# Block-sparse attention and a SoLU layer: start-up buffers, batch 1's order around a root, and the loads of the last two batches on ScalarE's queue

## The chip, the core and the metric

The kernel runs on one core of one Trainium2 chip. The metric is the device time of one execution in microseconds, from the runs shown; a second source is one profiled execution, whose records (the trace) say when each instruction of each engine started and ended, what it waited for, and when each DMA landed.

The engines work side by side and meet at semaphores: TensorE (PE; its weight loads are PEld), VectorE (DVE), ScalarE (ACT), GpSimd (POOL) and SyncE (SP). Each runs its own instructions strictly in order. SP and ACT can also issue DMAs; a DMA's issue is an instruction in the issuing engine's queue like any other.

## The reference

Two stages. Block-sparse attention over 4 batches, 8 heads, 768 positions, head size 64; then a SoLU layer over all 3072 rows:

```
scores = (q @ k.T) / sqrt(64)                 # masked per block of 32: window, edges, 3 random blocks
attn   = exp(scores - max) / (sum + 1e-9)
x      = attn @ v                             # reshaped to rows of 512
h      = x @ w_in                             # 512 -> 1024
solu   = h * softmax(h)
ln     = (solu - mean) / sqrt(var + 1e-6) * g_ln
out    = ln @ w_out                           # 1024 -> 512
```

The mask is the same for all heads and batches.

## The kernel before

Everything is cut into 144 slots. A pass is two blocks of 128 queries of one batch (12 passes, three per batch); a slot within a pass is one pair of heads and one third of the keys, so a pass has 12 slots. For each slot PE computes the scores (`scores`, L393: four matmuls of 256 columns into one of two PSUM tiles called sco), ACT takes the exponential of 1024 columns (`exps`, L407), and PE multiplies it with v (`outs`, L415). The mask rides along as 24 further rows of the transposed keys and queries (KT, QT), so no engine applies it. After the three slots of a pair, DVE takes a reciprocal and writes the normalised result xb (`normalise`, L435).

The SoLU layer of a pass runs during the next passes. xb is transposed by DMA (`x_turn`, xT; for the first pass on PE, `x_first`), then for each block of 128 rows: h on PE (`h_mms`), exp on ACT (`e_exp`, tile e), h times e on DVE (`solu`), a DMA transpose (`ln_turn`, lnT), statistics on DVE (`stats`), the root on POOL (`rstd`, L507, a power of -1/2), the last matmuls on PE (`o_mms`), a scaling on DVE (`scaled`, tile ot) and the store.

The inputs of a batch come as 12 loads of 384 KB (k, q and v of four pairs of heads, `load`, L309; batch 0 has the q loads split). They land in a ring of 7 staging tiles, POOL casts them to bf16 (`cast`). For batch 0 PE transposes k and q (`turn_mm`) and DVE copies them out (`turn_out`, L355); for later batches a DMA transposes them (`turn_dma`, tiles pd_k and pd_q) and POOL copies them into place (`shift`). KT, QT and VA exist twice and are used by alternate batches, and `mask_rows` puts the mask rows into the second copy once.

The order is written by hand. `at(when, fn, ...)` notes a step with a time in slots, and `emit` (L292) calls the steps sorted by that time; each engine gets its instructions in that order. So a number such as 30.05 places a step behind everything at or before 30.05 on its own engine, and nothing moves it later. The lists `first` (batch 1, L761) and `then` (batches 2 and 3, L766) hold the times of loads, casts, transposes, shifts, v loads and v casts; `t0` adds 36 slots per batch. Before the change all loads but the very first are issued from SP, whose queue also carries every DMA transpose and nearly every store.

The steps that the prediction follows: the filler matmuls that keep PE busy at the start (`zeros`, L600, tiles warm and warm_t), the mask tile m_ps and the copies of its rows to QT (L664), the loads of w_in (issued from POOL, L706), the first h matmul, and in slots 27 to 39 the roots, the mask copies (L735) and the casts of batch 1.

Of the kernel before, what the change touches and what calls it, by code (L numbers as in the profile page):

```python
# [7 lines left out]
FP32 = mybir.dt.float32  # L8
# [200 lines left out]
def kernel(  # L209
# [11 lines left out]
    nc = tc.nc  # L221

    B, H, S, D = q.shape
# [3 lines left out]
    TQ = 128  # L227
    NCH = S // TQ
# [11 lines left out]
    KR = D + NB  # L240
    PAIR = 2 * NCH
    PC = 2
    QW = PC * TQ
# [29 lines left out]
    KT = [fix.tile([128, H * NCH, TQ], BF16, name=f"KT{i}") for i in range(2)]  # L273
# [8 lines left out]
    p_sco = work.enter_context(tc.tile_pool(name="p_sco", bufs=2, space=bass.MemoryType.PSUM))  # L282
    p_op = work.enter_context(tc.tile_pool(name="p_op", bufs=1, space=bass.MemoryType.PSUM))
    p_h = work.enter_context(tc.tile_pool(name="p_h", bufs=1, space=bass.MemoryType.PSUM))
# [4 lines left out]
    def at(when, fn, *args):  # L289
        plan.append((when, len(plan), fn, args))  # L290
# [9 lines left out]
    def natural(b, pr, key):  # L300
        if key == "q":
            return qn[:, pr].rearrange("p c (h d) -> p c h d", h=2)
        r = KR if b == 0 and pr else D
        x0 = NCH * 2 * (D + (pr - 1) * KR) if pr else 0
        return kn[:, x0 : x0 + NCH * 2 * r].rearrange("p (c h r) -> p c h r", h=2, r=r)
# [12 lines left out]
    def copy(eng, o, i):  # L318
        if eng is nc.scalar:
            nc.scalar.copy(out=o, in_=i)  # L320
        else:
            eng.tensor_copy(out=o, in_=i)  # L322

    def cast(eng, b, pr, key, c0=0, c1=NCH, l0=None):
        l0 = c0 if l0 is None else l0
        st = stage[key, b, pr, l0].rearrange("p h (c d) -> p h c d", d=D)[:, :, c0 - l0 : c1 - l0, :]
        if key == "v":
            o = VA[b % 2][:, 2 * pr : 2 * pr + 2, c0:c1, 0:D]
        else:
            o = natural(b, pr, key)[:, c0:c1, :, 0:D].rearrange("p c h d -> p h c d")  # L330
        copy(eng, o, st)
# [23 lines left out]
    def turn_out(b, pr, key, engs, c0=0, c1=NCH):  # L355
        tp = turned.pop((key, b, pr, c0))
        dst = (KT if key == "k" else QT)[b % 2]
        for hh in range(2):
            h = 2 * pr + hh
            n, i = D, tp[hh * D : (hh + 1) * D] if len(tp.shape) == 2 else None  # L360
            if i is None:
                n, i = KR, tp[0:KR, hh]
            copy(engs[hh], dst[0:n, h * NCH + c0 : h * NCH + c1, :],
                 i[:, c0 * TQ : c1 * TQ].rearrange("p (c t) -> p c t", t=TQ))

    turned = {}

# [19 lines left out]
    def unit(s):  # L387
        ps, r = divmod(s, SLOTS)
        pr, u = divmod(r, UP)
        b, j = divmod(ps, NPB)  # L390
        return ps, b, j, pr, u
# [163 lines left out]
    DVE2 = (nc.vector, nc.vector)  # L555

    with tc.manual_schedule():
# [4 lines left out]
                          in_=bass.AP(tensor=_t32, offset=0, ap=[[2 * NR, NB], [1, 2 * NR]]))  # L562
# [7 lines left out]
        zer = fix.tile([128, 512], BF16, name="zer")  # L570
# [29 lines left out]
        def zeros(n, pool=p_o):  # L600
            w = pool
            if pool in (p_o, p_op):
                w = pool.tile([128, 512], FP32, tag="o" if pool is p_o else "op", name="warm")
            for _ in range(n):
                nc.tensor.matmul(w, zer[:, 0:128], zer, start=True, stop=True,
                                 skip_group_check=True)

        zeros(8)

        samp_f = fix.tile([NB, NR], FP32, name="samp_f")  # L610
        nc.vector.tensor_copy(out=samp_f, in_=samp_i[:, :, 0])
# [10 lines left out]
        for pr in range(1, NP):  # L622
            nc.scalar.activation(
                out=natural(0, pr, "k")[:, :, :, D:KR].rearrange("p c h r -> p (c h) r"),
                in_=zer[:, 0 : NCH * 2 * NB].rearrange("p (x r) -> p x r", r=NB),
# [1 line left out]
        cast(nc.scalar, 0, 0, "k", 0, 2, 0)  # L627
        cast(nc.scalar, 0, 0, "q", 0, 2, 0)
        cast(nc.scalar, 0, 0, "k", 2, NCH, 0)
        warm_t = p_sco.tile([128, 2, 512], FP32, tag="sco", name="warm_t")[:, 0, :]  # L630
        turn_mm(0, 0, "k", p_h, 0, 2)
        m_ps = p_sco.tile([TQ, 2, 512], FP32, tag="sco", name="m_ps")
        sel_f = selT.rearrange("p c t -> p (c t)")
        for i, x0, x1 in ((0, 0, QW), (1, QW, S)):
            nc.tensor.matmul(m_ps[0:KR, i, 0 : x1 - x0], mask_l, sel_f[:, x0:x1],
                             start=True, stop=True)
# [4 lines left out]
        def spread(x, n):  # L641
            return x.rearrange("p (o c) -> p o c", o=1).broadcast_to([NB, n, x.shape[-1]])
# [7 lines left out]
        def selector(pr):  # L650
            for base, sg in ((0, 1), (BLK - 1, -1)):
                o = natural(0, pr, "k")[:, :, :, D:KR]
                nc.gpsimd.affine_select(out=o, in_=o, compare_op=ALU.is_ge, fill=0.0, base=base,
                                        channel_multiplier=NCH * sg,
                                        pattern=[[sg, NCH], [0, 2], [-BLK * sg, NB]])
# [2 lines left out]
        mask_rows(nc.vector, KT[0], 0)  # L658
        turn_mm(0, 0, "q", p_o, 0, 2)
        turn_mm(0, 0, "k", p_op, 2, NCH)  # L660
        zeros(2, warm_t)
        turn_out(0, 0, "k", DVE2, 0, 2)
        for h0, n, i, x0, x1 in ((0, 2, 0, 0, QW), (0, 1, 1, QW, S), (1, 1, 1, QW, S)):
            nc.scalar.copy(out=rows(QT[0], h0, h0 + n)[:, :, x0:x1],  # L664
                           in_=spread(m_ps[D:KR, i, 0 : x1 - x0], n))
# [6 lines left out]
        scores(1)  # L672
        turn_mm(0, 1, "k", p_h)
        turn_mm(0, 1, "q", p_o, 0, 2)
        turn_out(0, 1, "k", DVE2)
        turn_out(0, 1, "q", DVE2, 0, 2)


        def turn(when, b, pr, key, pool, c0=0, c1=NCH, engs=DVE2, later=0.02):
            at(when, turn_mm, b, pr, key, pool, c0, c1)  # L680
            at(when + later, turn_out, b, pr, key, engs, c0, c1)
# [8 lines left out]
        for pr, w0, w1, w2 in ((2, 1.85, 2.805, 1.01), (3, 4.805, 5.805, 2.9)):  # L690
            at(w2, mask_rows, nc.vector, QT[0], 2 * pr)
            selector(pr)
            cast(nc.gpsimd, 0, pr, "k")
            cast(nc.gpsimd, 0, pr, "q", 0, 2)
            turn(w0, 0, pr, "k", p_h)
            turn(w1, 0, pr, "q", p_o, 0, 2)
        for pr in range(NP):
            at(2.0 + 0.1 * pr, cast, nc.gpsimd, 0, pr, "v")
            at(2.15 + 0.1 * pr, cast, nc.gpsimd, 0, pr, "q", 2, NCH)
        for pr, when in enumerate((8.9, 10.9, 12.9, 15.4)):  # L700
            turn(when, 0, pr, "q", p_o, 2, NCH, later=0.06)
        for n, when in ((2, 0.9), (1, 2.9), (1, 3.9)):
            at(when, zeros, n, p_op)
# [28 lines left out]

        at(2.05, w_load_in)
        at(9.0, w_load_out, 0, KF)
        for n, when in enumerate((7.0, 7.1, 13.1, 14.6, 16.1, 17.6, 30.2, 34.2)):  # L735
            at(when, mask_rows, nc.gpsimd if n < 2 else nc.vector, (KT[1], QT[1])[n % 2],
               2 * (n // 2))
        for c in range(KF):
# [7 lines left out]
        for s in range(n_units):  # L746
            ps, b, j, pr, u = unit(s)
# [10 lines left out]
        srcs = {"k": k, "q": q, "v": v}  # L758
        kq = [(key, pr) for pr in range(NP) for key in "kq"]
        vs = [("v", pr) for pr in range(NP)]  # L760
        first = (  # L761
# [4 lines left out]
        then = (  # L766
# [4 lines left out]
        for b in range(1, B):  # L771
            loads, casts, turns, shifts, v_loads, v_casts = first if b == 1 else then
            t0 = SLOTS * NPB * (b - 1)
            for (key, pr), t_l, t_c in zip(kq + vs, loads + v_loads, casts + v_casts):
                at(t0 + t_l, load, nc.sync, srcs[key], b, pr, key)
                at(t0 + t_c, cast, nc.gpsimd, b, pr, key)
            for (key, pr), t_t, t_s in zip(kq, turns, shifts):
                at(t0 + t_t, turn_dma, b, pr, key)
                at(t0 + t_s, shift, b, pr, key)


        def layer(ps, i, hs, es, os):
            for when, n0, n1 in hs:
                at(when, h_mms, ps, i, n0, n1)
            at(es, e_exp, ps, i)
            head = ps == 0 and i == 0
            at(es + (0.33 if head else 0.5), solu, ps, i)
            at(es + 0.55, ln_turn, ps, i)
            at(es + (6.6 if head else 3.4 if ps == 0 else 1.7), stats, ps, i)
            at(es + (6.7 if head else 3.5), rstd, ps, i)  # L790
            for when, n0, n1 in os:
                at(when, o_mms, ps, i, n0, n1)
            at(os[-1][0] + 0.1, scaled, ps, i, nc.vector)
            at(os[-1][0] + 0.12, store, ps, i)

        LP = NPASS - 1
        for ps in range(LP):
            b0 = SLOTS * (ps + 1)
            at(b0 + (1.9 if ps == 0 else -0.1), x_first if ps == 0 else x_turn, ps)
            if ps == LP - 1:  # L800
                break
            for i in range(PC):
                hs = b0 + 6 * i
                os = hs + (12 if ps == LP - 2 and i == PC - 1 else 14)
                layer(ps, i,
                      [(hs + 3.9, 0, 2), (hs + 4.85, 2, 3), (hs + 5.86, 3, 5), (hs + 6.85, 5, 7),
                       (hs + (7.79 if hs == SLOTS else 7.85), 7, 8)], hs + 8.5, [(os + 0.84, 0, 7), (os + 1.83, 7, 8)])


        ps, b0 = LP - 1, SLOTS * LP  # L810
# [177 lines left out]
```

## Time and profile before

| | us |
|---|---|
| median of 3 runs | 213.5 (211.46 to 215.09) |
| the profiled run's time | 212.79 |
| its span, first to last instruction | 211.1 |
| exps, 144 on ACT | 141.8 busy, 1.025 each |
| scores, 576 matmuls on PE | 86.4 busy |
| outs, 1152 matmuls on PE | 51.8 busy |
| h and o, 153 and 167 matmuls on PE | 48.8 and 41.8 busy |
| DMA issue to landing: loads of k, q, v | 5.4, 5.4, 6.1 (medians) |
| the same: lnT, xT, pd_k, pd_q | 4.1, 3.8, 2.8, 4.8 (medians) |

The granted clock of TensorE was 0.997 in the mean. In the page's lines, a group is given by line, engine and operation, written tile from read tile, shapes and count, then busy time and mean; after the last bar stands the idle time of the engine just before these instructions, and what ended it. In a timeline the two first numbers are the start and the length in us; the bracket at the end is the idle time before and what ended it. A queue with a q (SPq, ACTq) shows the sequencer's own work, such as issuing a DMA. PE's busy time counts matmuls that overlap, so it says more about waiting than about speed.

### The profile page before, as it was taken

Reading aid. Unit: us, or ns where it says so; the run is one execution under the profiler, and the core shown is the slowest. Engines: PE = TensorE matmul, PEld = TensorE weight load, DVE = VectorE, ACT = ScalarE, POOL = GpSimd, SP = SyncE. Lnnn points to the kernel's source line nnn. Section 1 sums busy time; section 2 is a strip of 40 time slices with the busy share of each in tenths; the row PEclk is TensorE's granted clock in tenths of the full one; section 3 lists DMA queues with packets and bytes.
Section 4 is the critical chain, followed back from the end, with each engine's and each line's share of the span. In section 5 each row is a group of like instructions: output and inputs, shape, how many; then the busy total and the mean of one; then the engine's idle time right before and its main releaser. Section 6 shows DMA issues by size and latency. Waiting matters only on the chain. (4 is left out here: it accounts for less than half of the span.)

```text
span 211.1 us, 5628 instructions
## 1 busy us (share of the span) xinstructions
PE 198.1 (94%) x2205; PEld 137.7 (65%) x2238; DVE 138.7 (66%) x329; ACT 176.0 (83%) x208; POOL 108.6 (51%) x154
## 2 busy tenths in 40 slices
PE   7899799998999999999999999999799999999991
PEld 2589667675666676676576676677476676665451
DVE  6785858968756557468548467557448557558782
ACT  6899779878889889889889889889779889876470
POOL 7799598788954483776353674594240110011111
PEclk9999999999999999999999999999999999999998
DMA  5999999999999879999998999989923285427404
GB/s 151 351 361 231 308 385 272 214 198 305 232 201 269 186 170 304 210 136 348 173 248 207 204 201 299 167 193 299 166 72 99 51 103 104 70 79 121 118 15 144
DMA packets 74291, 42.03 MB, mean 199 GB/s; under 512 B 56212, under 2 KB 69780, under 8 KB 74260
## 3 DMA queue, kind: packets, MB, share of 16 engines
q1 hardware_dynamic: 73316, 40.06, 82.2%
q0 software_dynamic: 528, 1.05, 2.8%
q10 hardware_dynamic: 416, 0.52, 0.8%
q8 instruction: 18, 0.29, 0.6%
q14 instruction: 13, 0.11, 0.2%
HBM read 23.07 MB, written 6.29 MB: 139 GB/s over the span
## 5 line engine op out<-in xcount | busy, mean ns | idle before, releaser
L411 ACT ACTIVATE exs<-sco 128x1024 bf16<-128x1024 f32 x144 | 141.8, 1025 | 10.2 <-PE sco L400 6.5
L400 PE MATMUL sco<-QT,KT 88*128 88x256 bf16 x576 | 86.4, 272 | 2.0 <-ACT QT L664 0.8
L400 PEld LDWEIGHTS <-KT 88*128 88x128 bf16 x576 | 55.1, 97 | 33.7 <-issue 5.3
L428 PE MATMUL op<-VA,exs 128*128 128x65 bf16 x1152 | 51.8, 194 | 0.3 <-DVE xb L442 0.2
L470 PE MATMUL h<-w_in_sb,xT 128*128 128x512 bf16 x153 | 48.8, 379 | 2.8 <-DVE solu L491 0.8
L428 PEld LDWEIGHTS <-exs 128*128 128x128 bf16 x1152 | 48.7, 97 | 3.5 <-DVE xb L442 0.7
L530 PE MATMUL o<-w_cen_sb,lnT 128*128 128x512 bf16 x167 | 41.8, 379 | 1.3 <-DMA lnT<-solu 1.1
L523 POOL TENSOR_TENSOR rstd<-vpe,mhalf 128x1 f32<-128x1 f32 x24 | 13.2, 549 | 49.3 <-DVE vpe L521 44.2
L441 DVE RECIPROCAL recip_all<-op 128x4 f32<-128x4 f32 x48 | 8.7, 182 | 41.5 <-PE op L428 41.1
L479 ACT ACTIVATE e<-h 128x1024 bf16<-128x1024 f32 x22 | 22.5, 1024 | 13.6 <-PE h L470 6.4
L505 DVE BATCH_NORM_STATS2 stats<-solu 128x6 f32<-128x512 bf16 x48 | 30.6, 680 | 0.0
L491 DVE TENSOR_TENSOR solu<-h,e 128x1024 bf16<-128x1024 f32 x22 | 26.8, 1216 | 4.1 <-ACT e L479 4.1
L322 POOL COPY KT<-pd_k 64x768 bf16<-64x768 bf16 x24 | 20.2, 840 | 13.1 <-DMA pd_k<-kn 12.3
L322 POOL COPY QT<-pd_q 64x768 bf16<-64x768 bf16 x24 | 19.8, 823 | 12.7 <-DMA pd_q<-qn 11.8
L530 PEld LDWEIGHTS <-lnT 128*128 128x128 bf16 x176 | 15.7, 98 | 14.9 <-DMA lnT<-solu 1.6
L541 DVE TENSOR_SCALAR ot<-o,rstd 128x512 f32<-128x512 f32 x20 | 15.0, 751 | 13.6 <-issue 6.8
L442 DVE TENSOR_TENSOR xb<-op,recip_all 128x256 bf16<-128x256 f32 x48 | 20.4, 425 | 1.7
L470 PEld LDWEIGHTS <-xT 128*128 128x128 bf16 x176 | 15.3, 98 | 6.6 <-DMA xT<-xb 2.0
L322 POOL CAST qn<-st_q 128x768 bf16<-128x768 f32 (+2 forms) x19 | 14.2, 747 | 6.2 <-DMA st_q<-in_q_dram 6.0
L322 POOL CAST kn<-st_k 128x768 bf16<-128x768 f32 x15 | 12.4, 826 | 8.4 <-DMA st_k<-in_k_dram 8.2
L322 POOL CAST VA<-st_v 128x768 bf16<-128x768 f32 x16 | 13.2, 831 | 4.6 <-DMA st_v<-in_v_dram 4.1
L717 POOL TENSOR_SCALAR w_out_sb<-w_out_f,g_ln_sb 128x512 bf16<-128x512 f32 x8 | 6.3, 802 | 2.5 <-DMA w_out_f<-in_moe_w_out_dram 2.5
(87 smaller groups left out, 111.0 us busy)
## 6 DMA issues: line engine op xcount, KB each, us to landing
st_v<-in_v_dram SPq DMA_DIRECT2D x16, 384.0 KB, 6.1
out_dram<-ot SPq DMA_DIRECT2D x23, 256.0 KB, 3.9
st_k<-in_k_dram SPq DMA_DIRECT2D x15, 384.0 KB, 5.4
st_q<-in_q_dram SPq DMA_DIRECT2D x12, 384.0 KB, 5.4
w_out_f<-in_moe_w_out_dram SPq DMA_DIRECT2D x4, 512.0 KB, 11.9
st_q<-in_q_dram SPq DMA_DIRECT2D x4, 256.0 KB, 7.1
w_in_sb<-in_moe_w_in_dram POOLq DMA_DIRECT2D x1, 1024.0 KB, 12.4
st_q<-in_q_dram SPq DMA_DIRECT2D x4, 128.0 KB, 4.9
```

The lines of the kernel that those rows point to most:

```text
L322: eng.tensor_copy(out=o, in_=i)
L400: nc.tensor.matmul(sco[:, hh, kk * QW : (kk + 1) * QW], KT[b % 2][0:KR, h * NCH + 2 * u + kk, :], QT[b % 2][0:KR, h * NCH + PC * j : h * N ...
L411: nc.scalar.activation(out=exs_of[ps, pr][:, u].rearrange("p a b c -> p (a b c)"), in_=sco_of.pop(s).rearrange("p a b -> p (a b)"), func=A ...
L428: nc.tensor.matmul(op[:, hh, ic, :], exs[:, u, hh, kk, ic * TQ : (ic + 1) * TQ], VA[b % 2][:, 2 * pr + hh, 2 * u + kk, :], start=(u == 0 a ...
L442: nc.vector.tensor_tensor(out=xb_of[ps][:, :, 2 * pr * D : 2 * (pr + 1) * D].rearrange("p c (h d) -> p h c d", h=2), in0=op[:, :, :, 0:D], ...
L470: nc.tensor.matmul(h_of[ps, i][:, half, :], xT_of[ps][:, i * KD + c, :], w_in_sb[:, c, half * HF : (half + 1) * HF], start=(c == 0), stop= ...
L479: nc.scalar.activation(out=o, in_=h, func=ACT.Exp, scale=1.0, accum_out=esum_all[:, t : t + 1])
L491: nc.vector.tensor_mul(out=so, in0=h, in1=e)
L505: nc.vector.bn_stats(out=stat_of[ps, i][:, half, :], in_=so[:, half, :])
L523: nc.gpsimd.tensor_tensor(out=rstd_of[ps, i], in0=vpe, in1=mhalf, op=ALU.pow)
L530: nc.tensor.matmul(ops_of[ps, i], lnT_of[ps, i][:, c, :], w_cen_sb[:, c, :], start=(c == 0), stop=(c == KF - 1), skip_group_check=True)
L541: nc.vector.tensor_scalar(out=o, in0=i_, scalar1=r, scalar2=None, op0=ALU.mult)
```

## The change

Four parts.

The start: the eight filler matmuls write a tile of the score pool instead of the o pool, the two fillers before the first scores become four of half the width and write an unused half of the mask tile's first bank, and the copies of the transposed k of pairs 1 to 3 of batch 0, one per head with all 768 columns, become one for both heads with the first 256 columns and, behind the q copies, one for both heads with the other 512 (`k_out`).

The middle of batch 0: the last q turn goes from slot 15.4 to 15.9 and `x_first` from 13.9 to 14.4; the mask rows of pair 3 of the second KT and QT go from 30.2 and 34.2 to 39.0 and 39.5.

Batch 1: casts of k3, q3 and v1 go from 27.6, 27.7 and 28.5 to just behind the root at 30.0, the shifts of k2 and q2 from 30.05 and 30.1 to 30.1 and 30.15, a transpose from 33.0 to 33.2, and the scaling and store of the first block of rows from slot 27.9 to 29.87.

Batches 2 and 3: their 24 loads are issued from ScalarE's queue, at the same times of the plan.

```diff
+    def k_out(pr, c0, c1):
+        tp = turned["k", 0, pr, 0]
+        nc.vector.tensor_copy(
+            out=KT[0][0:KR].rearrange("p (h c) t -> p h (c t)", c=NCH)[
+                :, 2 * pr : 2 * pr + 2, c0 * TQ : c1 * TQ],
+            in_=tp[0:KR, :, c0 * TQ : c1 * TQ])
...
-        zeros(8)
+        warm_t = p_sco.tile([128, 2, 512], FP32, tag="sco", name="warm_t")[:, 0, :]
+        zeros(8, warm_t)
...
-        zeros(2, warm_t)
+        for _ in range(4):
+            nc.tensor.matmul(m_ps[:, 0, QW : 2 * QW], zer[:, 0:128], zer[:, 0:QW], start=True,
+                             stop=True, skip_group_check=True)
...
-        turn_out(0, 1, "k", DVE2)
+        k_out(1, 0, 2)
         turn_out(0, 1, "q", DVE2, 0, 2)
+        k_out(1, 2, NCH)
...
-            turn(w0, 0, pr, "k", p_h)
+            at(w0, turn_mm, 0, pr, "k", p_h)
+            at(w0 + 0.02, k_out, pr, 0, 2)
             turn(w1, 0, pr, "q", p_o, 0, 2)
+            at(w1 + 0.03, k_out, pr, 2, NCH)
...
-        for pr, when in enumerate((8.9, 10.9, 12.9, 15.4)):
+        for pr, when in enumerate((8.9, 10.9, 12.9, 15.9)):
...
-        for n, when in enumerate((7.0, 7.1, 13.1, 14.6, 16.1, 17.6, 30.2, 34.2)):
+        for n, when in enumerate((7.0, 7.1, 13.1, 14.6, 16.1, 17.6, 39.0, 39.5)):
...
-            [9.1, 9.2, 9.3, 9.4, 9.5, 9.6, 27.06, 27.07], [9.5, 9.6, 14.0, 14.1, 14.2, 14.3, 27.6, 27.7],
-            [12.5, 12.6, 24.05, 24.06, 27.1, 27.2, 33.0, 36.1],
-            [17.0, 17.1, 26.0, 27.3, 30.05, 30.1, 36.6, 39.0],
-            [9.7, 27.08, 27.3, 27.4], [18.0, 28.5, 32.0, 33.0])
+            [9.1, 9.2, 9.3, 9.4, 9.5, 9.6, 27.06, 27.07], [9.5, 9.6, 14.0, 14.1, 14.2, 14.3, 30.05, 30.06],
+            [12.5, 12.6, 24.05, 24.06, 27.1, 27.2, 33.2, 36.1],
+            [17.0, 17.1, 26.0, 27.3, 30.1, 30.15, 36.6, 39.0],
+            [9.7, 27.08, 27.3, 27.4], [18.0, 30.07, 32.0, 33.0])
...
-                at(t0 + t_l, load, nc.sync, srcs[key], b, pr, key)
+                at(t0 + t_l, load, nc.sync if b == 1 else nc.scalar, srcs[key], b, pr, key)
...
-            at(os[-1][0] + 0.1, scaled, ps, i, nc.vector)
-            at(os[-1][0] + 0.12, store, ps, i)
+            out_at = 29.87 if head else os[-1][0] + 0.1
+            at(out_at, scaled, ps, i, nc.vector)
+            at(out_at + 0.02, store, ps, i)
...
-            at(b0 + (1.9 if ps == 0 else -0.1), x_first if ps == 0 else x_turn, ps)
+            at(b0 + (2.4 if ps == 0 else -0.1), x_first if ps == 0 else x_turn, ps)
```

More of the change, by code (lines that the diff above doesn't have):

```diff
@@ L359, in turn_out @@
             h = 2 * pr + hh
[L360 to L364, printed above, removed]
+            copy(engs[hh], dst[0:D, h * NCH + c0 : h * NCH + c1, :],
+                 tp[hh * D : (hh + 1) * D, c0 * TQ : c1 * TQ].rearrange("p (c t) -> p c t", t=TQ))
+    def k_out(pr, c0, c1):
[4 more added lines that the diff above has]
+            in_=tp[0:KR, :, c0 * TQ : c1 * TQ])
     turned = {}
@@ L629 @@
         cast(nc.scalar, 0, 0, "k", 2, NCH, 0)
-        warm_t = p_sco.tile([128, 2, 512], FP32, tag="sco", name="warm_t")[:, 0, :]
         turn_mm(0, 0, "k", p_h, 0, 2)
```

## The prediction

> **What bounds it.** I read the page first, then the waits by engine, then the stretches, then the timelines around each wait of TensorE.
>
> ```profile
> PE 198.1 (94%) x2205; PEld 137.7 (65%) x2238; DVE 138.7 (66%) x329; ACT 176.0 (83%) x208; POOL 108.6 (51%) x154
> ```
>
> TensorE is busy 94% of the span; ScalarE, which gets the loads, 83%. A busy PE is not a PE at its peak, so the stretches matter more (us, then busy time of each engine, granted clock, DMA share, GB/s):
>
> ```profile
> 72.43:80.11 7.68, 7.63 (x89) 5.39 (x89) 4.69 (x12) 6.93 (x10) 5.98 (x8) 1.00 0.86 204
> 149.46:158.45 8.99, 8.25 (x90) 5.62 (x92) 4.68 (x12) 7.04 (x10) 2.19 (x3) 1.00 0.55 99
> ```
>
> These are six slots each, from one exps to the sixth after it. In the first PE fills 7.63 of 7.68 us; from exps 45 to exps 141 nearly every period is 7.67 to 7.70. So the floor is PE's own work, and only what exceeds 7.68 can be won: I find 0.6 in exps 27 to 33, 0.7 in 33 to 39, 0.5 in 39 to 45, 0.25 in 75 to 81, 1.3 in 111 to 117 (the second line) and 0.4 in 135 to 141. The waits of PE (total, times, longest) say on whom:
>
> ```profile
> PE o L530 <- DMA lnT<-solu: 1.1, 2, 0.9
> PE h L470 <- DVE solu L491: 0.8, 1, 0.8
> PE h L470 <- DMA w_in_sb<-in_moe_w_in_dram: 0.4, 1, 0.4
> ```
>
> **The beginning.** As built, scores(0) no longer waits for all three copies of the mask rows (L664, 5.62 to 7.17 us) but for the first, at about 6.2; the second score tile takes over the wait for the last. Exps(0) is then held by ScalarE's own copies, to about 7.2 instead of 7.85: 0.65 us won. The fillers are the same columns (2 x 512 become 4 x 256): 0. The split copies put 512 of 1536 columns of each k pair ahead of the q copies: the pair of 88x768 copies took 1.02 us, so about 0.4 us stands ahead of q in place of 1.02, and some 0.4 of the 0.65 lives on. Then it meets a wall: in PE's timeline the first h matmul stands at 26.34, on w_in's DMA.
>
> ```profile
> 25.35 0.60 PE L400 MATMUL sco<-QT,KT 88*128 88x256 bf16 x4
> 26.34 0.38 PE L470 MATMUL h<-w_in_sb,xT 128*128 128x512 bf16 x1 [0.38 <-DMA w_in_sb<-in_moe_w_in_dram]
> ```
>
> That DMA is issued from POOL at 13.88, after casts that wait for loads and for neither PE nor ScalarE, and it lands at the same 26.3. PE only arrives earlier and waits longer. The same holds for moving the turn of q3 behind one group of scores (its 0.37 us wait for DVE goes). Net 0; bounds -0.4 (the landing moves too) and +0.3 (a dearer copy shows). The cover is the w_in wait.
>
> **The root and batch 1.** On POOL the second root (rstd) now stands ahead of the casts of k3, q3 and v1; on DVE the first ot stands behind a reciprocal and xb, and two mask copies (0.55 us each) go from 48.17 and 52.06 to after slot 38's xb. DVE's and PE's timelines:
>
> ```profile
> 44.86 0.75 DVE L541 TENSOR_SCALAR ot<-o,rstd 128x512 f32<-128x512 f32 x1 [1.57 <-POOL rstd L523]
> 48.17 0.55 DVE L647 COPY KT<-selT 24x1536 bf16<-24x1536 bf16 x1
> ```
> ```profile
> 46.22 0.68 PE L428 MATMUL op<-VA,exs 128*128 128x65 bf16 x16 [0.17 <-DVE xb L442]
> 50.59 0.60 PE L470 MATMUL h<-w_in_sb,xT 128*128 128x512 bf16 x2 [0.77 <-DVE solu L491]
> ```
>
> DVE sat 1.57 us before ot while xb, which PE wanted, was queued behind. With xb first PE starts its outs at 45.88 (the scores before it at 45.44 take 0.435), not 46.22: 0.34. Solu at 49.32 stands behind that delay and the mask copy, 0.8 us together; it then ends before PE needs the bank: 0.77. The third place is h at 58.79, 0.35 on xT: xT can go some 0.7 us earlier, but a mask copy now stands before the solu that frees the bank (solu ended at 58.01, now +0.57), so I take 0.2. POOL: kn3's cast moves from 47.30 to about 48.2, the k2 shifts no later than their 51.20, since the root is out of the way. What is late next is the pair-3 shift of q (59.60 to 61.31, wanted by the scores at 62.39): 1.1 us of cover. Sum -1.3; bounds -1.7 and -0.4.
>
> **The 24 loads: the queue left.** SP's queue in the last batches, then PE's wait:
>
> ```profile
> 140.00 1.64 SPq L313 DMA_DIRECT2D st_v<-in_v_dram x3
> 143.30 1.24 SPq L496 DMA_TRANSPOSE lnT<-solu  x1
> ```
> ```profile
> 150.00 1.68 PE L530 MATMUL o<-w_cen_sb,lnT 128*128 128x512 bf16 x7 [0.91 <-DMA lnT<-solu]
> ```
>
> This lnT took 6.7 us from issue to landing; the median is 4.1. Four loads were ahead of it. On ScalarE they are reached after exps 99, 100 and 101 (134 to 137 us), 4 us sooner, and are through before 143. That period's excess of 1.3 us (0.91 here, the rest at the h behind it) goes: -1.3; bounds -1.3 and 0. By the Trainium skill ("DMA: Bandwidth & Descriptors", Issuing engines are not separate DMA queues) another issuer saves only the issuing time, which SP has to spare: by that rule this term would be 0 and the sum 1.3 higher, which is "nothing left" below. This trace speaks against it: the lnT did wait behind loads on its own queue.
>
> **The 24 loads: the queue entered.** Each stands after exps 39, 40, 41, 41, 51, 52, 53, 53, 63, 64, 65, 65 and the same plus 36, so in the three that run back to back after an e. SP paid 0.40 to 0.85 us per load from 59 us on. ScalarE's sequencer runs ahead of its engine:
>
> ```profile
> 0.92 1.28 ACT L250 ACT_TABLE_LOAD   x1 [0.92 <-PEq L972]
> 0.96 0.44 ACTq L313 DMA_DIRECT2D st_k<-in_k_dram  x1
> ```
>
> The issue ran inside the table load. An exps lasts 1.02 us and the next starts 0.90 to 1.04 after it, so one issue of 0.5 is covered; two after exps 41 take 1.1 and make the next some 0.1 to 0.2 late. The scores of slot s+2 start 0.05, 0.22, 0.46, 0.56 us after exps(s) ends (first to fourth after an e), which covers that. So 0; upper bound by SP's transpose issues (1.24 us), below.
>
> Queued behind a load are all later exps. Each load waits for its buffer's cast (done slots before) and, as built, for the DMA eight places before it, which shares its semaphore. Most of those landed long before; the thin ones are v0 and k3 of batch 2 (they wait for an xT and a pd_q that landed at 73.97 and 74.88; ScalarE gets there at 74.3 and 74.8) and their like 36 and 48 slots on. Landings half a us later would still be covered by the 0.56.
>
> **Loads beside transposes.** Before, FIFO kept the loads behind the boundary's transposes; now they run together. Landing to use, in the trace: xT 0.05 to 0.7 us, lnT 0.04 to 3.9. What a foreign packet does is seen here (GB/s in 40 slices of 90 to 94 us):
>
> ```profile
> GB/s 218 212 212 193 67 5 0 10 95 207 202 195 195 371 138 41 3 0 0 0 0 0 0 5 10 8 10 10 8 10 18 251 294 289 292 255 287 289 289 287
> ...
> q8 instruction: 1, 0.02, 1.5%
> ...
> lnT<-solu SPq DMA_TRANSPOSE x1, 4.5
> ```
>
> One instruction fetch, and the transposes stand for 1.5 us. Lower bound 0. Upper: all four loads of a cluster (about 1.05 us each by their landings, 4.2) pass its last transpose; against slacks of 0.05 to 2.7 that is up to 2 us in each of six clusters, +12. I take one load's time per cluster, as the nearest row is FIFO behind one load: it shows where slack is under 1.05, at exps 63 (lnT, 0.8), 75 (xT 0.05, and the q shift at 108.25 for scores at 108.69) and 99 (xT): 0.25 + 0.95 + 0.3, say +1.5.
>
> The same page (Queues, rings and completion order) has each DMA engine take turns between queues by whole packets; by that rule lnT would pass among the loads and the term would lie under +1.5. No transpose of this trace ran beside a load of another queue.
>
> **Sum.** The profiled run took 212.79 us (span 211.1 and 1.7 around it). 0 - 1.3 - 1.3 + 0 + 1.5 = -1.1: 211.7. The median of the runs is 0.7 above the profiled run, so 212.4.
>
> **Rivals.**
> *ScalarE held* (slower): a load at the head of its queue stops the exps. If an issue beside SP's transposes takes their 1.24 us, the exps of a cluster come 0.4, 0.8 and 2.3 us late (1.24 and some 0.06 of waits against 0.90 each; the pair adds 1.5), and against 0.22, 0.46 and 0.56 plus 0.14 of room PE loses about 1.7: six clusters 10, less 2.6: 221. It decides from about 0.75 us per issue, where the pair overruns 1.04 + 0.56. For: SP issues transposes without a break at 72 to 76 and 86 to 91. Against: at 0.96 both queues issued at once in 0.44.
> *Transposes late* (slower): 1.5 us in each cluster, 9 less 2.6: about 219; half of that, 215. For: the stall above. Against: most lnT have 1 to 3 us.
> *Nothing left*: what DVE gives back is eaten by xT, the next in line, and the loads were hidden anyway: 213.5. For: xT lands within 0.2 us of its use at five of eight boundaries.
> *All won*: no contention, w_in lands early, the 0.25 at exps 81 goes too: -0.4 -1.7 -1.3 -0.3 -0.6 (xT) = 208.5 to 209.2.
> That the loads don't come sooner is not a case: they stand 3 to 5 us ahead of SP's times.
>
> **Numbers.** Forecast 0.46; nothing left 0.20; all won 0.07; ScalarE held 0.12; transposes late 0.15, half of it over the bound. A change under about 2% (209.2 to 217.8) can't be told from none here. Faster 0.05, within 0.75, slower 0.20. Range 209.5 to 218.5, leaving out most of "all won", of "ScalarE held" and the worst of the transposes; the forecast's own range is 211 to 214.
>
> **What would show it.** PE without waits at 46 and 50, and at the o after the last v loads; h still waiting for w_in at about 26.3, now over 0.38; exps intervals of 0.90 across each load issue of about 0.5 us. Wrong, if exps wait for a DMA, if an issue on ScalarE's queue lasts over 0.75, or if PE waits for lnT, xT or a q shift at 79, 94, 105 or 108 us.

## The result, and the profile after

| | us |
|---|---|
| before, median of 4 runs | 213.56 (211.46 to 215.09) |
| after, median of 4 runs | 234.9 (232.99 to 237.95) |
| ratio | 1.1005, 95% interval 1.0872 to 1.1139 |
| profiled run after, its span | 234.52, 232.9 |

Slower by 10%, far outside the range. The ratios, here and below, compare the executions within about 1.5% of each kernel's fastest, and the medians are of all. Lines of the changed kernel stand 4 to 10 further down: exps is L415, scores L404, outs L432, h L474, o L534, the xT transpose L457, lnT L500.

The page's table of engines after:

```profile
PE 206.9 (89%) x2240; PEld 141.5 (61%) x2240; DVE 137.2 (59%) x329; ACT 175.3 (75%) x208; POOL 107.0 (46%) x154
```

TensorE now idles for 26 us of its span instead of 13, and its busy time itself rose by 8.8 us for the same matmuls (198.1 before; of the 35 records more, 33 are matmuls that the trace of before lacks and 2 are fillers cut in half). Both need a cause. The waits of PE, then those of ScalarE (total, times, longest):

```profile
PE sco L404 <- ACT exs L415: 7.6, 5, 4.1
PE o L534 <- DMA lnT<-solu: 6.5, 4, 3.2
PE h L474 <- DMA xT<-xb: 2.6, 1, 2.6
PE h L474 <- DMA w_in_sb<-in_moe_w_in_dram: 1.4, 1, 1.4
```
```profile
ACT exs L415 <- DMA pd_q<-qn: 4.8, 1, 4.8
ACT exs L415 <- DMA pd_k<-kn: 2.5, 1, 2.5
...
ACT QT L670 <- PE m_ps L666: 0.9, 1, 0.9
```

The transposes lnT and xT come late (PE waited 1.1 and 0.35 us for them before), and twice an exps, which reads nothing that a DMA brings, waits for the transpose of a q or k. PE's timeline places the waits:

```profile
61.33 0.60 PE L474 MATMUL h<-w_in_sb,xT 128*128 128x512 bf16 x2 [2.59 <-DMA xT<-xb]
85.31 1.01 PE L404 MATMUL sco<-QT,KT 88*128 88x256 bf16 x4 [4.12 <-ACT exs L415]
108.78 1.69 PE L534 MATMUL o<-w_cen_sb,lnT 128*128 128x512 bf16 x7 [2.32 <-DMA lnT<-solu]
143.86 2.58 PE L534 MATMUL o<-w_cen_sb,lnT 128*128 128x512 bf16 x7 [3.21 <-DMA lnT<-solu]
```

Each stands behind one of the six clusters of loads. The stretches (six slots each, columns as before the change: us, busy time of each engine, granted clock, DMA share, GB/s):

```profile
56.23:68.92 12.69, 9.93 (x91) 6.42 (x92) 5.90 (x14) 7.03 (x10) 7.37 (x10) 0.87 1.06 228
76.60:90.39 13.79, 9.67 (x88) 6.36 (x87) 4.39 (x10) 6.82 (x10) 6.28 (x10) 0.75 1.18 203
106.82:116.91 10.09, 8.13 (x91) 5.70 (x92) 4.68 (x12) 7.04 (x10) 5.62 (x8) 1.00 0.87 168
141.00:153.67 12.67, 9.81 (x91) 6.20 (x92) 4.70 (x12) 7.05 (x10) 5.48 (x8) 0.87 0.71 131
153.67:164.00 10.33, 8.52 (x88) 5.89 (x87) 4.83 (x10) 6.85 (x11) 4.05 (x6) 0.88 1.04 273
170.00:177.70 7.70, 7.70 (x90) 5.42 (x89) 4.70 (x12) 6.95 (x9) 2.19 (x3) 1.00 0.60 132
```

Without loads a stretch still takes 7.7 us (last line). The five above it, each with a wait of 1.8 us or more, take 10 to 14. In four of them the same 88 to 91 matmuls are busy for 8.5 to 9.9 us at a granted clock of 0.75 to 0.88. In the third line, whose wait is the 2.32 us at 108.78, the clock stays 1.00. Two pieces of the first two stretches show what the mean hides:

```profile
62.60:65.90 3.30, 3.30 (x27) 2.10 (x24) 1.00 (x5) 1.92 (x2) 1.64 (x2) 0.50 1.17 259
83.10:89.80 6.70, 4.49 (x31) 2.98 (x31) 0.00 (x0) 3.39 (x4) 3.96 (x6) 0.50 1.22 191
```

The trace's clock records have four such pieces at 0.50 before the kernel's end, three of 3.4 us and this one of 6.8, each beginning in a wait or within 1.5 us of its end. So most of these waits are paid twice, as idle time and as slower matmuls behind it.

How exps 54 came to wait for pd_q is seen in ScalarE's timeline with its queue:

```profile
78.36 0.38 ACTq L313 DMA_DIRECT2D st_v<-in_v_dram  x1
78.41 1.04 ACT L415 ACTIVATE exs<-sco 128x1024 bf16<-128x1024 f32 x1
83.76 0.38 ACTq L313 DMA_DIRECT2D st_k<-in_k_dram  x1
84.24 1.94 ACT L415 ACTIVATE exs<-sco 128x1024 bf16<-128x1024 f32 x2 [4.80 <-DMA pd_q<-qn]
```

The load of k3 stands between the exps. In the trace it has the same semaphore as this pd_q, the DMA that the prediction put eight places before it, and it waits for it. That transpose's issue ended at 77.26 and it landed at 83.67, 6.4 us later. The load is issued at 83.76, and only then go the exps queued behind it. An issue itself takes 0.37 to 0.66 us on ScalarE.

### The profile page after: what moved, and what is told of

Its sections match the earlier page's. It is cut to its first block, busy times and chain, and to the rows that moved or that the text cites. A ratio compares the mean times of both kernels' runs of the same rounds, so it can differ in the third digit from the quotient of the medians.

```text
span 232.9 us, 5692 instructions
## 1 busy us (share of the span) xinstructions
PE 206.9 (89%) x2240; PEld 141.5 (61%) x2240; DVE 137.2 (59%) x329; ACT 175.3 (75%) x208; POOL 107.0 (46%) x154
## 3 DMA queue, kind: packets, MB, share of 16 engines
q0 software_dynamic: 528, 1.05, 2.4%
## 4 chain that ended last, share of the span: by engine, by line
PE 59%; DMA 28%; DVE 4%; POOL 3%; ACT 1%; issue 1%; SPq 1%; ACTq 0%; POOLq 0%; DVEq 0%
PE sco L404 20%; PE o L534 13%; PE h L474 13%; PE op L432 11%; DMA lnT<-solu 10%; DMA w_in_sb<-in_moe_w_in_dram 6%; DMA pd_k<-kn 4%; DMA pd_q<-qn 3%; DMA xT<-xb 3%; DMA st_k<-in_k_dram 2%; PE he L851 1%; POOL kn L322 1%; DVE solu L495 1%; POOL kn L657 1%; DVE stats L509 1%
## 5 line engine op out<-in xcount | busy, mean ns | idle before, releaser
L415 ACT ACTIVATE exs<-sco 128x1024 bf16<-128x1024 f32 x144 | 141.1, 1024 | 30.6 <-PE sco L404 18.5
L404 PE MATMUL sco<-QT,KT 88*128 88x256 bf16 x576 | 89.4, 278 | 8.8 <-ACT exs L415 7.6
L404 PEld LDWEIGHTS <-KT 88*128 88x128 bf16 x576 | 56.5, 99 | 43.4 <-issue 17.2
L474 PE MATMUL h<-w_in_sb,xT 128*128 128x512 bf16 x176 | 57.0, 389 | 4.0 <-DMA xT<-xb 2.6
L432 PE MATMUL op<-VA,exs 128*128 128x65 bf16 x1152 | 53.1, 196 | 0.0
L534 PE MATMUL o<-w_cen_sb,lnT 128*128 128x512 bf16 x176 | 46.9, 390 | 6.5 <-DMA lnT<-solu 6.5
L432 PEld LDWEIGHTS <-exs 128*128 128x128 bf16 x1152 | 50.1, 99 | 3.2 <-ACT exs L415 0.4
L322 POOL COPY KT<-pd_k 64x768 bf16<-64x768 bf16 x24 | 20.0, 832 | 34.2 <-DMA pd_k<-kn 33.0
L534 PEld LDWEIGHTS <-lnT 128*128 128x128 bf16 x176 | 16.1, 100 | 21.1 <-DMA lnT<-solu 7.0
L474 PEld LDWEIGHTS <-xT 128*128 128x128 bf16 x176 | 15.9, 100 | 8.6 <-DMA xT<-xb 3.1
L322 POOL CAST qn<-st_q 128x768 bf16<-128x768 f32 (+2 forms) x19 | 13.5, 713 | 0.8 <-DMA st_q<-in_q_dram 0.3
L726 POOL TENSOR_SCALAR w_out_sb<-w_out_f,g_ln_sb 128x512 bf16<-128x512 f32 x8 | 5.7, 721 | 3.3 <-DMA w_out_f<-in_moe_w_out_dram 3.2
## 6 DMA issues: line engine op xcount, KB each, us to landing
st_q<-in_q_dram SPq DMA_DIRECT2D x4, 384.0 KB, 10.3
```

The lines of the kernel that those rows point to most:

```text
L404: nc.tensor.matmul(sco[:, hh, kk * QW : (kk + 1) * QW], KT[b % 2][0:KR, h * NCH + 2 * u + kk, :], QT[b % 2][0:KR, h * NCH + PC * j : h * N ...
L415: nc.scalar.activation(out=exs_of[ps, pr][:, u].rearrange("p a b c -> p (a b c)"), in_=sco_of.pop(s).rearrange("p a b -> p (a b)"), func=A ...
L432: nc.tensor.matmul(op[:, hh, ic, :], exs[:, u, hh, kk, ic * TQ : (ic + 1) * TQ], VA[b % 2][:, 2 * pr + hh, 2 * u + kk, :], start=(u == 0 a ...
L474: nc.tensor.matmul(h_of[ps, i][:, half, :], xT_of[ps][:, i * KD + c, :], w_in_sb[:, c, half * HF : (half + 1) * HF], start=(c == 0), stop= ...
L534: nc.tensor.matmul(ops_of[ps, i], lnT_of[ps, i][:, c, :], w_cen_sb[:, c, :], start=(c == 0), stop=(c == KF - 1), skip_group_check=True)
```

## The experiments

**Which part of the change.** Two kernels take it apart. The first is the changed kernel with one word put back:

```diff
-                at(t0 + t_l, load, nc.sync if b == 1 else nc.scalar, srcs[key], b, pr, key)
+                at(t0 + t_l, load, nc.sync, srcs[key], b, pr, key)
```

> The changed kernel, with the 24 loads of the last two batches back on SyncE's queue; the edits of the beginning and of the root stay. Theory (the loads, running beside SP's transposes from a second queue, cost about 25 us; the start costs about 0.9, the root wins about 1.3): 213 us, ratio 0.99 to 1.003, exps intervals of 39 to 51, 51 to 63 and their like back at before's within 0.3, and the lnT wait of 0.9 at about 150 us back. Rival (the edits of the beginning and the root shift the work of batches 1 to 3 and cost the time): 220 or more.

Measured: 213.73 (10 runs), ratio to before 1.0027 (0.9972 to 1.0082). The second is the kernel of before with that one word changed the other way:

```diff
-                at(t0 + t_l, load, nc.sync, srcs[key], b, pr, key)
+                at(t0 + t_l, load, nc.sync if b == 1 else nc.scalar, srcs[key], b, pr, key)
```

> The kernel of before, with one word changed: the 24 loads go through ScalarE's queue. Theory (loads beside transposes): 234 to 237 us, with the stretches of exps 39 to 45, 51 to 57, 69 to 75 and 93 to 99 longer by 3 to 6 us each as in the changed kernel. Rival (the other edits are needed for the loss, or make up half of it): under 225.

Measured: 233.13, ratio 1.0947 (1.083 to 1.1064). The loads' queue is the whole loss, within these intervals; the rest of the change comes to nothing that can be measured. What that rest does is seen in the first kernel's PE timeline:

```profile
58.50 0.60 PE L474 MATMUL h<-w_in_sb,xT 128*128 128x512 bf16 x2 [1.15 <-DMA xT<-xb]
```

Exps 27 to 39 take 1.26 us less than before, as forecast, but the next h then waits 1.15 us for an xT that comes hardly earlier (58.45, before 58.74), and exps 39 to 45 take 9.25 us instead of 8.20.

**Is it the time at which the loads run, or ScalarE's queue?** Loads still on ScalarE's queue, moved by up to 2.2 slots:

```diff
-            [3.2, 4.1, 5.0, 5.9, 15.2, 16.1, 17.9, 27.2], [8.2, 9.4, 10.6, 11.8, 20.2, 21.4, 23.8, 32.2],
+            [5.2, 5.3, 6.2, 6.3, 17.2, 17.3, 18.3, 29.2], [8.2, 9.4, 10.6, 11.8, 20.2, 21.4, 23.8, 32.2],
...
-            [17.0, 28.1, 29.0, 29.9], [22.6, 33.4, 34.6, 35.8])
+            [18.2, 29.3, 30.2, 30.3], [22.6, 33.4, 34.6, 35.8])
```

> The changed kernel, the loads still on ScalarE's queue, but moved by up to 2.2 slots to places where SP's queue has no transpose by the trace of the changed kernel (slots 5.2 to 6.3, 17.2 to 18.3, 29.2 to 30.3 of each batch). Theory (what costs is that loads run in time beside transposes): 212 to 215, PE's waits for lnT and xT back under 2 us in sum. Rival (ScalarE's queue itself costs, as its exps are held behind loads wherever these stand): 222 or more, ScalarE waits for DMAs stay above 4 us in sum. Between: both.

Measured: 226.03 (214.29, 225.40, 226.66, 232.22). The lowest execution fits the theory, the other three the rival's number, and in the profiled one (225.40) no exps waits for a DMA, so this run decides nothing by itself. The edit didn't do what it was meant to: an lnT is issued in each gap, and one of them (issued at 79.45 us) landed 7.7 us after the end of its issue, beside all four loads of a cluster.

**Another issuer.** The same loads at the same places of the program, from GpSimd:

```diff
-                at(t0 + t_l, load, nc.sync if b == 1 else nc.scalar, srcs[key], b, pr, key)
+                at(t0 + t_l, load, nc.sync if b == 1 else nc.gpsimd, srcs[key], b, pr, key)
```

> The changed kernel, with the 24 loads at their same places in the program but issued from GpSimd's queue, which uses other semaphores and holds no exps. Theory (loads beside transposes, whoever issues them): 222 or more, with PE's waits for lnT and xT of 4 us or more in sum and no wait of ScalarE for a DMA other than through the scores. Rival (the harm is that ScalarE's exps are held behind loads): 214 to 217, lnT and xT land as in before.

Measured: 218.29 (two executions, 215.80 and 220.78). In the profiled one, 220.78, exps 39 to 117 take 105.4 us against 102.5 with the loads on SP, and another 3.7 us of its length lie ahead of exps 39, before any moved load (58.96 against 55.21). This spoke for the rival, ScalarE's hold. But the trace shows a second difference. POOL comes to the loads later than ScalarE did: its first issue of the cluster starts at 64.50, 5.5 us after exps 39, where ScalarE's started 0.9 us before it, and by then xT and lnT of this boundary had landed (61.98, 64.43). So the loads were moved again, still from GpSimd, but 4.3 slots earlier in the program:

```diff
-                at(t0 + t_l, load, nc.sync if b == 1 else nc.scalar, srcs[key], b, pr, key)
+                at(t0 + t_l - (4.3 if b > 1 else 0), load, nc.sync if b == 1 else nc.gpsimd, srcs[key], b,
+                   pr, key)
```

> The changed kernel with the 24 loads on GpSimd's queue, as in the run before with that queue, but written 4.3 slots earlier in the program, so that they are issued about when ScalarE issued them, beside the batch boundary's transposes, instead of some 4 to 9 us later. ScalarE still holds nothing. Theory (the time in which loads and transposes run together costs, about 0.6 us for each us of it, whoever issues): exps 39 to 117 takes 112 us or more instead of 105.4, 223 to 232. Rival (the hold of ScalarE by a load that waits for a semaphore is needed for the loss): 214 to 219, as with the later loads.

Measured: 238.33 (233.16 to 249.28), as slow as the changed kernel, and exps 39 to 117 take 121.8 us instead of 105.4. Its waits of PE:

```profile
PE o L534 <- DMA lnT<-solu: 6.5, 5, 3.7
PE sco L404 <- POOL QT L322: 6.5, 4, 4.9
PE h L474 <- DMA xT<-xb: 2.6, 3, 1.2
```

LnT and xT cost what they cost in the changed kernel (6.5 and 2.6). The hold of ScalarE is gone, and in its place the scores wait for the shifts: the longest, 4.9 us, for one whose pd_q landed 10.1 us after the end of its issue. The hold was one outlet of the lateness, not its cause.

**One cluster less.** The changed kernel with k2, q2, v0 and k3 of each batch on SP:

```diff
-                at(t0 + t_l, load, nc.sync if b == 1 else nc.scalar, srcs[key], b, pr, key)
+                at(t0 + t_l, load, nc.sync if b == 1 or 15.0 < t_l < 18.0 else nc.scalar, srcs[key], b, pr, key)
```

> The changed kernel with the second cluster of each batch (k2, q2, v0, k3, at slots 15 to 18) back on SyncE's queue, and the other 16 loads on ScalarE's; the long waits of ScalarE for pd_q and its kin (4.8 and 2.5 us) stood in clusters with v0 and k3 or the last v. Theory (late landings cost at every cluster, the hold of ScalarE is only one way in which they are felt): about 222 to 228, with the stretch of exps 51 to 57 back at 7.7 to 8.5, and 39 to 45 still at 12 or more. Rival (the hold of ScalarE is the whole loss): 213 to 217.

Measured: 224.13 (220.11 to 226.47). Exps 51 to 57 are back at 7.68, 39 to 45 still take 12.03, with no exps waiting for a DMA there. So a cluster costs by itself, and without a hold too.

**The queue or the order?** Loads on SP's own queue, ahead of the transposes instead of behind them:

```diff
-                at(t0 + t_l, load, nc.sync if b == 1 else nc.scalar, srcs[key], b, pr, key)
+                at(t0 + t_l - (4.3 if b > 1 else 0), load, nc.sync, srcs[key], b, pr, key)
```

> The changed kernel with the 24 loads on SyncE's own queue, but written 4.3 slots earlier, ahead of the transposes that they stood behind. One queue, so no turns between queues. Theory (what counts is which packets go ahead of a transpose, the second queue only changed that): a cluster of four loads ahead of xT or lnT makes it 3 to 5 us late, 220 to 232. Rival (it takes two queues at once): 212 to 216, as the queue is as full as before and nothing runs beside a transpose.

Measured: 224.05, ratio to before 1.051 (1.0444 to 1.0575), against 1.0027 with the loads 4.3 slots later on the same queue. PE's timeline:

```profile
58.28 1.68 PE L534 MATMUL o<-w_cen_sb,lnT 128*128 128x512 bf16 x7 [2.02 <-DMA lnT<-solu]
62.41 0.60 PE L474 MATMUL h<-w_in_sb,xT 128*128 128x512 bf16 x2 [1.80 <-DMA xT<-xb]
...
80.70 0.60 PE L474 MATMUL h<-w_in_sb,xT 128*128 128x512 bf16 x2 [2.75 <-DMA xT<-xb]
```

No second queue is needed for about half of the loss: it is enough that loads go ahead of xT and lnT. Not all of that is bytes. The first xT is issued 1.1 us after exps 39 starts, where with the loads behind it that was 1.2 us before: two loads' issues, of 0.43 and 1.38 us, now stand ahead of it on SP. From the end of its issue it then takes 3.4 us, against 3.1. The second xT takes 3.9 from there, against 2.0.

**The cost by itself.** A kernel of DMAs alone, in stretches that VectorE gates:

> Not the computation: the output is written as zeros. It measures the disputed cost by itself. Seven stretches, each gated by VectorE behind the one before, all twice: four DMA transposes of 128x768 bf16 on SyncE's queue; four loads of 384 KB on ScalarE's queue; both at once from the two queues; the four loads and then the four transposes on SyncE's one queue; the eight in turn on SyncE's queue; transposes on SyncE's and loads on GpSimd's queue at once; four loads on SyncE's and four on ScalarE's queue at once. Theory (a transpose and a load of two queues slow each other): alone about 5.5 to 7 and 5 to 6 us; both at once from two queues clearly more than the sum of the two alone, 15 us or more, and more than in turn on one queue (11 to 13). Rival (two queues only share the bandwidth): both at once takes no more than the sum, 10 to 12 us, and less than on one queue; transposes then are only late by the bytes that pass between.

Worked out from the DMAs' issue and landing times in its trace, two repeats:

| stretch | first issue to last landing, us | a transpose: end of issue to landing, us |
|---|---|---|
| 4 transposes, SP | 6.8, 6.7 | 1.5 to 1.6 |
| 4 loads, ScalarE | 7.7, 6.8 | |
| both at once, two queues | 10.3, 9.6 | 2.2 to 6.1 |
| loads, then transposes, SP | 10.5, 11.0 | 1.5 to 5.3 |
| in turn, SP | 11.5, 11.8 | 1.5 to 3.5 |
| both at once, SP and GpSimd | 11.5, 11.4 | 3.4 to 6.6 |
| 4 loads SP, 4 loads ScalarE | 10.7, 12.1 (the second beside the output's stores) | |

My theory at this point (15 us or more, two queues slow each other) was wrong: both at once take no longer than in one queue, rather less. What changes is who waits. VectorE's timeline has a copy that waits for each transpose; the first two alone (issues from 86.14 us), then the first two beside the loads (from 100.95):

```profile
88.95 0.14 DVE L37 CAST junk<-dst 1x1 f32<-1x1 bf16 x1 [2.57 <-DMA dst<-src]
90.27 0.14 DVE L37 CAST junk<-dst 1x1 f32<-1x1 bf16 x1 [1.17 <-DMA dst<-src]
...
106.55 0.14 DVE L37 CAST junk<-dst 1x1 f32<-1x1 bf16 x1 [5.43 <-DMA dst<-src]
109.31 0.14 DVE L37 CAST junk<-dst 1x1 f32<-1x1 bf16 x1 [2.62 <-DMA dst<-src]
```

The first transpose arrives 2.8 us after the first issue when alone, and 5.6 us beside loads. The packet records show why. Counted in the first repeat of "both at once", over all 16 DMA engines (a load has 256 packets of 1536 B, a transpose 768 of 256 B, and its completion 32 of 4 B):

```
from to (us)     load packets   transpose packets   transpose completions
28.40 to 30.25        199                0                     0
30.25 to 31.25         57              726                     0
31.25 to 32.25        234               42                     0
32.25 to 32.50         50                0                    30
```

Load 1 passes whole, then transpose 1, then load 2, and only behind load 2 the completion of transpose 1, whose data had all gone out a microsecond before. Here the queues take turns by blocks about as long as a DMA (further on, from 33.5 us, the blocks are shorter), so a transpose can pay for a load twice: before its data and before its completion.

**Bytes or issues?** Each moved load cut to a sixth, with its cast:

```diff
+        c1 = 1 if b > 1 else c1
         eng.dma_start(
-            out=st.rearrange("p h (c d) -> p h c d", d=D),
+            out=st.rearrange("p h (c d) -> p h c d", d=D)[:, :, 0 : c1 - c0, :],
```

> The changed kernel with each of the 24 loads of the last two batches, and its cast, cut to the first of its six row blocks: 256 packets of 256 B instead of 1536 B, so batches 2 and 3 compute with stale rows. Issues on ScalarE's queue and their waits for semaphores stay. New theory, from the runs so far (two queues take turns by packets: the 48 or 64 packets of 256 B that a transpose has on each DMA engine alternate with the 16 of 1536 B of each load in flight, so a transpose beside four loads lands with the last of them): packets of about 20 ns instead of 74 leave under 1.3 us per cluster, 212 to 217. Rival (the issues on ScalarE's queue and their waits cost by themselves): 225 or more.

Measured: 215.92, ratio 1.0084 (1.0034 to 1.0133). With the issues and their semaphores in place and the bytes gone, about a tenth of the loss is left. Two things limit this: the smaller casts also relieve GpSimd, and in the profiled execution (216.92, above the median) PE still waits 2.1 us for one xT and exps 1.0 us for one pd_q.

**Fewer at a time.** Loads on ScalarE's queue, some two slots apart:

```diff
-            [3.2, 4.1, 5.0, 5.9, 15.2, 16.1, 17.9, 27.2], [8.2, 9.4, 10.6, 11.8, 20.2, 21.4, 23.8, 32.2],
+            [0.2, 2.2, 4.2, 6.2, 12.2, 14.2, 18.2, 25.2], [8.2, 9.4, 10.6, 11.8, 20.2, 21.4, 23.8, 32.2],
...
-            [17.0, 28.1, 29.0, 29.9], [22.6, 33.4, 34.6, 35.8])
+            [16.2, 27.2, 29.2, 31.2], [22.6, 33.4, 34.6, 35.8])
```

> The changed kernel, the loads on ScalarE's queue, but spread so that they stand some two slots apart (0.2, 2.2, 4.2, 6.2, 12.2, 14.2, 16.2, 18.2, 25.2, 27.2, 29.2, 31.2 of each batch) instead of in clusters of four; casts as they were. Theory of turns by packets: a transpose then alternates with the 16 packets of one load, about 1.2 us later instead of 4 to 5, and most of that has slack: 214 to 220. Rival (any plain load beside a transpose stalls the queue for some fixed time): each of the 24 loads meets a transpose now, 225 or more.

Measured: 228.75, ratio 1.0529 (1.0444 to 1.0615): my forecast of 214 to 220 fell. No exps waited for a DMA. The worst place in PE's timeline of the profiled execution, the slowest of the six (235.06):

```profile
67.08 1.03 PE L474 MATMUL h<-w_in_sb,xT 128*128 128x512 bf16 x2 [5.18 <-DMA xT<-xb]
```

This xT was issued at 58.26, with the loads of q0 (58.04) and k1 (59.50) beside it, and more than their two microseconds went by: from 62.75 to 65.5 us, but for half a microsecond, the packets moved at 20 to 101 KB/us, where 290 and more is usual beside it. Steps of a quarter microsecond at under 120 KB/us with the DMA engines over 80% busy, from 55 us to 30 us before the end, come to 18.0 us before the change, 18.8 with the loads back on SP, 21.0 in the changed kernel and 21.0 here. So standstills belong to these transposes anyway; with loads beside them, more DMAs can stand in one. The prediction had laid one to an instruction fetch. Before the change, 10 of the 12 fetches of that time are followed within 1.5 us by a standstill of half a microsecond or more, and 10 of 17 such standstills follow one; in the changed kernel it is 8 of 12 and 8 of 22. The one at 62.75 here follows none (the last fetch began at 60.6). So a fetch often goes before one, and it is not the whole cause, which was not found.

**A version for both gains.** Since the edits around the root were eaten by an xT behind two v loads on one queue, those loads were moved behind it (loads on SP):

```diff
-            [9.7, 27.08, 27.3, 27.4], [18.0, 30.07, 32.0, 33.0])
+            [9.7, 27.08, 36.15, 36.2], [18.0, 30.07, 39.1, 39.2])
```

> The changed kernel with the 24 loads back on SyncE's queue and, new, the loads of v2 and v3 of batch 1 moved from slot 27.3 behind the xT and the last q transpose of the batch (36.15), their casts from 32.0 and 33.0 to 39.1. With the loads on SyncE the root and the casts won 1.3 us up to exps 39, and the h behind it gave 1.15 back, waiting for an xT that stood behind these two loads on the one queue. Theory (the queue's order is what the next wait hangs on): that wait goes, exps 39 to 45 takes 7.7 to 8.3 instead of 9.25, 212 to 212.8, ratio to before 0.990 to 0.998. Rival (xT is late by its own transposes, or the casts and lnT pay for the move): no change against the kernel without it, ratio 1.000 to 1.006.

Measured: 212.74 (12 runs), ratio 1.0021 (0.9981 to 1.0061): no gain that can be told. The stretch after exps 39, in its table of stretches, and PE's timeline there:

```profile
55.69:64.15 8.46, 7.79 (x89) 5.33 (x89) 6.10 (x14) 6.93 (x10) 5.67 (x8) 1.00 0.93 259
```
```profile
58.20 0.59 PE L474 MATMUL h<-w_in_sb,xT 128*128 128x512 bf16 x2 [0.62 <-DVE solu L495]
```

The xT wait is gone and the stretch 0.8 us shorter than 9.25, but behind xT stood solu, which frees h's bank.

**All together.** Exps 39 to 117 in each profiled run (13 stretches; 13 times 7.68 is 99.8), with the time in it in which load packets and transpose packets both moved (quarter microseconds in which each took 3% or more, counted from the packet records). The beginning is left out, since some of these executions started 4 to 5 us late, before any moved load:

| kernel | profiled execution, us | exps 39 to 117, us | loads and transposes together, us |
|---|---|---|---|
| before | 212.79 | 101.9 | 8.0 |
| loads back on SP | 212.00 | 102.5 | 8.5 |
| GpSimd | 220.78 | 105.4 | 16.8 |
| second cluster on SP | 220.11 | 110.6 | 24.8 |
| shifted by up to 2.2 slots | 225.40 | 110.5 | 29.0 |
| two slots apart | 235.06 | 120.8 | 36.3 |
| changed kernel | 234.52 | 124.0 | 42.3 |
| before, loads alone on ScalarE | 238.20 | 127.6 | 43.8 |
| GpSimd, 4.3 slots earlier | 239.09 | 121.8 | 27.8 |
| SP, 4.3 slots earlier | 224.80 | 113.8 | 13.0 |

Each row is one execution, and the kernels with late transposes scatter much more than the one before (214 to 232 us for the shifted loads). The first eight go up together, but for one tie. The last two don't lie on that line: overlap alone doesn't set the cost. That it is decided by which transpose the loads go ahead of is argued from these two rows, and not shown transpose by transpose.

## Why the prediction was wrong

**Loads beside transposes** is the step that failed: +1.5 stood in the sum. Exps 39 to 117 take 124.0 us in the changed kernel and 102.5 with the loads back on SP, so the clusters cost 21.5, beyond my upper bound of 12. Three things went into it.
- The price was one load's time once per cluster, from the nearest row, FIFO behind one load. A cluster is four loads, issued when xT, pd_q, pd_k and lnT of the boundary are under way, and each transpose pays anew: four lnT, issued at 58, 79, 100 and 134 us, landed 7.7, 5.7, 7.5 and 8.8 us after the end of their issues, where the median before was 2.3.
- I drew the wrong side from a rule that stood beside the sum. By the Trainium skill (DMA: Bandwidth & Descriptors, section Queues, rings and completion order) a DMA engine drains a whole packet of some 9 to 17 descriptors, at most 64, from one queue before it turns to the next. The DMA kernel agrees in kind: at its start blocks of 16 load packets and 48 transpose packets per engine took turns. From this I had concluded that lnT would pass among the loads. But turns are a loss for whoever was alone on the queue before, and FIFO had put the transposes first.
- I counted waits only. Their echo, the granted clock of 0.75 to 0.88 behind them, shows in PE's busy time: 206.9 us against 197.6 with the loads on SP, 9.3 us. PE was busy for 14.8 of the 17 us at half clock; if all of that took twice as long as it had to, it is 7.4 of the 9.3, by my estimate.

"That the loads don't come sooner is not a case: they stand 3 to 5 us ahead of SP's times" saw the fact and took it for a gain. It was the harm: 4.3 slots earlier cost 11 us on SP's own queue and 16 from GpSimd (113.8 against 102.5, 121.8 against 105.4, exps 39 to 117).

**The queue entered** (0) failed with it. The hidden issue held: 0.37 to 0.66 us, under the 0.75 at which it was to decide. "Landings half a us later would still be covered" was the weak point, and the thin load was named rightly, k3 of batch 2; its pd_q landed 6.4 us after the end of its issue, and ScalarE stood for 4.80, later for 2.48 behind a v load.

**The rivals.** "ScalarE held" (221) had the right sign and place and the wrong mechanism: no long issue in this kernel, but a load waiting for a late DMA (with the loads moved by up to 2.2 slots an issue took up to 1.5 us). "Transposes late" (219) was the right mechanism at a fraction of its size. "Nothing left" was right for the root: xT was next in line.

**The queue left** (-1.3): exps 111 to 117 take 7.68 instead of 8.99, the time that was forecast, but mostly not for its reason. With the loads still on SP they take 7.91, so only about 0.2 of the 1.3 was the queue's, nearer to the 0 of "nothing left".

**The root and batch 1** (-1.3): -1.26 between exps 27 and 39, and then 1.05 given back between 39 and 45 in the kernel with the loads on SP. I named the pair-3 shift of q as next to be late. At the third place I counted 0.2 us as won; instead the h at 58.50 waited 1.15 for xT.

**The beginning** (0): exps(0) starts at 8.03, not 7.2, as the mask row copies now wait 0.9 for the fillers that write into m_ps, a wait I overlooked. It made no difference, for the reason given: the h at 26.34 waits for w_in. In the changed kernel that DMA landed at 27.23 instead of 26.30 and all is 0.9 later; with the old beginning and the loads alone moved it landed at 26.92, with the new beginning and the loads on SP at 26.22, so it does not follow that edit; why it was late stays open.

Two of the signs that were to show the prediction wrong came: exps waited for a DMA, and PE waited for lnT and xT. Not tried by a run of its own: how the 21.5 us divide between late lnT and xT, late shifts, the hold and the clock, and why the second queue costs about twice what the changed order on SP costs.

## What to carry over

A queue that holds both urgent transposes and bulk loads is a priority list. Moving the loads to another queue saved no bandwidth here, it took away the order: before doing so, list which transposes are under way when the other engine reaches the issue, and price each of them by the loads beside it. And an issue on a compute engine carries waits that its code doesn't show, here for the DMA that shares its semaphore; they can cost as much as that DMA is late.

## What was not expected of the hardware

- Two queues at once are no slower in sum than one (9.6 to 10.3 us against 10.5 to 11.8), but the completion of a transpose whose data was through came a microsecond later, behind a whole load of the other queue.
- At waits of 1.8 to 4.1 us TensorE's granted clock went to 0.50 for 3.4 or 6.8 us, and the same matmuls took 8.5 to 9.9 us instead of 7.6; at one wait of 2.32 us it stayed 1.00.
- With transposes under way the DMA engines go through standstills of up to 2.3 us with few bytes moved, about as much before the change (18.0 us of 126) as after it (21.0 of 148), and many begin within 1.5 us of an instruction fetch.
